# Another sharing rule for the helper operations up to tile 25, and a global transpose that is issued one place later

## The chip, the cores and the metric

The kernel runs on one core of a Trainium2 chip. A core has a matrix engine (TensorE, PE in the profile; its weight loads are the row PEld), three engines for elementwise work (VectorE or DVE, ScalarE or ACT, GpSimdE or POOL) and a queue for transfers on SyncE (SP). The metric is the device time in microseconds, the median of the runs of a kernel; lower is better.

## The reference

Two steps follow each other. First an attention over 8 batches and 8 heads with head size 64, in which each sequence has 32 global and 512 local tokens: a global query sees every key, a local query sees the 32 global keys and the local keys at most 32 positions away.

```
s_g = scale * q_g @ k_all.T            out_g = softmax(s_g) @ v_all
s_l = concat(scale * q_l @ k_g.T, where(|i-j| <= 32, scale * q_l @ k_l.T, -1e9))
out_l = softmax(s_l) @ concat(v_g, v_l)
```

Then the 8 x 544 outputs, heads side by side (512 wide), go through a dense layer with three weight matrices and a maximum, and through a second one:

```
h = max(x @ w1, x @ w2, x @ w3)        # 512 -> 768
out = h @ w_out                        # 768 -> 512
```

All data are float32.

## The kernel before

**Precision.** Outside of the first 20 tiles, a float32 operand is split in two parts: a copy rounds it to the matrix engine's fast format, and a subtraction leaves the remainder as a second operand in the same format. The matrix engine multiplies the parts (three products for the dense layers). Each split is thus one copy and one subtraction of the same width: `split_q`, `split_v`, `split_k`, `split_x`, and the same pair inside `convert` (weights, which come as 64-bit patterns of a wider type and take four VectorE instructions before the pair, lines 161 to 166), `layer1` (the hidden layer h) and `trans`/`transg`. The first 20 tiles (`NATK`, `NAT`) multiply the unsplit float32 operands, which takes no split but is slower on the matrix engine.

**Tiles.** A tile is 128 local queries of two heads of one batch; there are 128 tiles, four to a pair of heads (t = 0 to 3) and 16 to a batch. The main loop (`for i, sl in enumerate(SEQ)`) does for tile i: the transposes of the probabilities of tile i+1 (`trans`, four transposes into the only PSUM tile T, then a copy and a subtraction into the operand `pt`), some matmuls of the dense layer of the batch before (`fill(n)`: the generator in `mm[0]` issues n of them), the scores and softmax of tile i+3 (`scores`), more dense matmuls, the product with the values (`pv`), for t = 0 and 1 the scores of the global queries of the next pair (`glob`), for t = 2 their softmax (`glob_soft`), 3 dense matmuls, the transpose of the global probabilities of tile i+1 (`transg`: one transpose into a PSUM tile S, then a copy and a subtraction into columns 128 to 160 of `pt`), 7 dense matmuls, `split_v`, loads, and in the first 24 tiles a step of the weight conversion. `scores`, `glob` and `transg` share the two PSUM tiles S. A tile has 21 dense matmuls up to i = 31 and 18 after that. `pv` of a tile needs both `trans` and `transg` of that tile.

**Softmax.** `scores` reduces on VectorE (line 325), takes the exponential on ScalarE (327), adds a constant and takes the reciprocal on VectorE (330, 331), and multiplies the 128 x 192 or 128 x 224 probabilities of each of the two heads by it (`times`, lines 111 to 115). In the first 16 tiles the transposes read the result directly (tensor `early`); from tile 16 on it takes a transfer (`prob<-s`) into the operand format first.

**Who does a helper operation.** Three helpers pick their engine while the program is written: `sub` (VectorE or GpSimdE), `copy` (VectorE or ScalarE) and `times` (any of the three). `load` keeps a sum of estimated nanoseconds for each engine ("a", "d", "p"); `least` gives an operation to the engine whose sum, with the operation's cost added, is the smallest; `spend` books work with a fixed engine; `settle(4500)`, once a tile, lifts each sum to at least the largest one less 4500. GpSimdE cannot read PSUM, so operations that read PSUM are for VectorE or ScalarE. Line 97 in the profile is the instruction of `sub`, 103 and 105 are those of `copy` on VectorE and ScalarE, 111, 113 and 115 those of `times` on VectorE, ScalarE and GpSimdE. The program's order on each engine is in the main the order in which the loop issues the instructions; a list scheduler puts an instruction whose operands it expects late behind later ones that it expects ready.

Of the kernel before, what the change touches and what calls it, by code (L numbers as in the profile page):

```python
# [50 lines left out]
def f32(ap):  # L51
    return ap.bitcast(F32)


def body(ctx, tc, kin, qin, vin, min_, win, out):
# [12 lines left out]
    small = ctx.enter_context(tc.tile_pool(name="small", bufs=2))  # L68


    load = {"a": 0.0, "d": 0.0, "p": 0.0}

    def width(ap):
        n = 1
        for x in ap.shape[1:]:
            n *= x
        return n

    def spend(e, ns):
        load[e] += ns  # L80

    def least(costs):
        e = min(costs, key=lambda e: load[e] + costs[e])
        load[e] += costs[e]
        return e

    def settle(ns):
        top = max(load.values()) - ns
        for e in load:
            load[e] = max(load[e], top)  # L90

    def sub(out, a, b, psum=False):
        n = width(out)
        c = {"d": n * 1.04 + (160 if psum else 110)}
        if not psum:
            c["p"] = n * 2.32 + 130
        (dve if least(c) == "d" else pool).tensor_tensor(out=out, in0=a, in1=b, op=ALU.subtract)  # L97

    def copy(out, a, psum=False):
        n = width(out)  # L100
        c = {"d": n * (1.04 if psum else 0.52) + (160 if psum else 150), "a": n * 0.833 + (150 if psum else 190)}
        if least(c) == "d":
            dve.tensor_copy(out=out, in_=a)
        else:
            act.copy(out=out, in_=a)  # L105

    def times(out, a, col):
        n = width(out)
        e = least({"d": n * 0.52 + 125, "a": n * 0.833 + 185, "p": n * 1.27 + 150})
        if e == "d":  # L110
            dve.tensor_scalar(out=out, in0=a, scalar1=col, scalar2=None, op0=ALU.mult)
        elif e == "a":
            act.activation(out=out, in_=a, func=AF.Copy, scale=col)
        else:
            pool.tensor_scalar(out=out, in0=a, scalar1=col, scalar2=1.0, op0=ALU.mult, op1=ALU.mult)  # L115
# [13 lines left out]
    def clear():  # L129
        for t in (*probg, qgz):  # L130
            pool.memset(f32(t), 0.0)
# [3 lines left out]
    def weight(n, a):  # L135
        return wt[n][:, 512 * a:512 * a + 512]
# [17 lines left out]
    def convert(n):  # L154
        r = raw[n].bitcast(I32).rearrange("p (n t) -> p n t", t=2)
        if n < 18:
            c = spare[n // 2 % 2 if n < 15 else 1][:, n % 2]
        else:
            c = moe.tile([128, 512], I32, name="wct", tag="o", bufs=2)
        marks[n] = act.activation(out=f32(c), in_=f32(r)[:, :, 1], func=AF.Abs).ins.name  # L160
        dve.tensor_scalar(out=f32(c), in0=f32(c), scalar1=2.0 ** -15, scalar2=HIMAX, op0=ALU.max, op1=ALU.min)
        dve.tensor_scalar(out=c, in0=c, scalar1=0x07FFFFFF, scalar2=3, op0=ALU.bitwise_and, op1=ALU.logical_shift_left)
        spend("a", 520)
        yield
        dve.scalar_tensor_tensor(out=c, in0=r[:, :, 1], scalar=-0x40000000, in1=c, op0=ALU.bitwise_and, op1=ALU.bitwise_or)
        dve.scalar_tensor_tensor(out=c, in0=r[:, :, 0], scalar=29, in1=c, op0=ALU.logical_shift_right, op1=ALU.bitwise_or)
        spend("d", 1900)
        yield
        wt[n] = const.tile([128, 1024], F32R, name=f"w{n}", tag=f"w{n}")
        copy(weight(n, 0), f32(c))  # L170
        sub(weight(n, 1), f32(c), f32(weight(n, 0)))
        yield
# [20 lines left out]
    EARLY = 16  # L193
# [144 lines left out]
    def trans(sl):  # L338
        if sl >= NS:
            return  # L340
        s = sc.pop(sl)
        ps, n = turned, WIN[sl % 4][1] - 128
        pr, ident = (ps, one) if sl < EARLY else (ps.bitcast(F32R), identr)
        for j in range(2):
            pe.transpose(pr[:, 256 * j:256 * j + 128], s[:, j, 0:128], ident)  # L345
            pe.transpose(pr[0:n, 256 * j + 128:256 * j + 256], s[:, j, 128:128 + n], ident)  # L346
        src = ps.rearrange("p (x q) -> p x q", q=128)
        if sl < NAT:
            pt = pts[sl] = att.tile([128, 2, 2, 160], F32, name="pt", tag="pt")
            copy(pt.rearrange("p j c q -> p (j c) q")[:, :, 0:128], src, True)  # L350
        else:
            pt = pts[sl] = att.tile([128, 2, 2, 2, 160], F32R, name="pt", tag="pt")
            v = pt.rearrange("p j c a q -> p (j c) a q")
            copy(v[:, :, 0, 0:128], src, True)
            sub(v[:, :, 1, 0:128], src, f32(v)[:, :, 0, 0:128], True)

    def transg(sl):
        if sl >= NS:
            return
        p, t = divmod(sl, 4)  # L360
        pt = pts[sl]
        i, h, n = GCH[t]
        g = psS.tile([128, 512], F32, name="S")
        pe.transpose(g.bitcast(F32R)[:, 0:128], probg[p % 2][:, i], identr)  # L364
        src = g[:, 64 * h:64 * h + 64 * n].rearrange("p (c j g) -> p c j g", j=2, g=SG)
        if sl < NAT:
            copy(pt.rearrange("p j c q -> p c j q")[:, 0:n, :, 128:160], src, True)
            return
        v = pt.rearrange("p j c a q -> p c j a q")
        hi, lo = v[:, 0:n, :, 0, 128:160], v[:, 0:n, :, 1, 128:160]  # L370
        copy(hi, src, True)
        sub(lo, src, f32(hi), True)
# [66 lines left out]
    def layer2(hh, n, stores):  # L439
        for t in range(n // 128):  # L440
            ps = pm.tile([128, 512], F32, name="pm")
            q = 0
            for f in range(6):
                for a, w in ((0, 0), (1, 0), (0, 1)):
                    pe.matmul(ps, lhsT=hh[f][:, a, 128 * t:128 * t + 128], rhs=weight(18 + f, w), start=(q == 0), stop=(q == 17))  # L445
                    q += 1
                    if q < 18:
                        yield
            o = moe.tile([128, 512], F32, name="o", tag="o", bufs=2)
            copy(o, ps, True)  # L450
            stores(t, o)
            yield
# [3 lines left out]
    def moe_local(b):  # L456
        def st(t, o):
            r = b * TOK + SG + t * 128
            nc.sync.dma_start(out=out[r:r + 128], in_=o)
        x, hh = xs[b], []  # L460
        for c0, n in ((0, 256), (256, 256)) if b == 0 else ((0, 512),):
            yield from layer1(x, hh, c0, n)
        yield from layer2(hh, SL, st)
# [45 lines left out]
    def fill(n):  # L509
        if mm[0]:  # L510
            for _ in range(n):
                next(mm[0], None)
# [3 lines left out]
    def tile_at(i):  # L516
        return SEQ[i] if i < NS else NS
# [30 lines left out]
    for i, sl in enumerate(SEQ):  # L548
        p, t = divmod(sl, 4)
        b = p // NP  # L550
        settle(4500)
        if i % 16 == 0 and b > 1:
            fill(400)
            mm[0] = moe_local(b - 1)
        trans(tile_at(i + 1))
        first = i < 32
        fill(6 if first else 4)
        next_scores(i + 3)
        if i < 16:
            if i == 7:  # L560
                clear()
            if i in (10, 12):
                load_k((i - 2) // 2)
            if i == 14:
                split_k(5)
                load_k(6)
        elif t == 3:
            split_k(p + 2)
            load_k(p + 3)
        fill(5 if first else 4)  # L570
        pv(sl)
        if i >= 12:
            if t <= 1 or i in (12, 13):
                glob(p + 1 if i >= 16 else 4, t if i >= 16 else i - 12)
            elif t == 2 or i == 14:
                glob_soft(p + 1 if i >= 16 else 4)
        fill(3)
        if i + 1 >= EARLY:
            transg(tile_at(i + 1))
        fill(7)  # L580
        split_v(tile_at(i + 2))
        if i < 12:
            load_v(tile_at(i + 4), i + 4)
        else:
            load_v(tile_at(i + 4))
        for _ in range(WS[i] if i < len(WS) else 0):
            weight_step()
        if i < 16:
            if i % 2:
                if i < 8:  # L590
                    xs.setdefault(0, []).append(x_tile())
                split_x(xr[p][:, 2 * (i // 8):2 * (i // 8) + 2, 0:128], xs[0][p], 256 * (i // 8), 256)
            if i == 7:
                mm[0] = moe_local(0)
        elif i % 16 >= 12:
            q = b * NP + i % 16 - 12
            xs.setdefault(b, []).append(x_tile())
            split_x(xr[q][:, :, 0:128], xs[b][-1], 0, SL)
# [66 lines left out]
```

## Time and profile before

| | |
|---|---|
| median of three runs | 860.33 us (859.11 to 861.30) |
| the profiled execution, its own time | 859.92 us |
| span of its trace | 858.0 us |
| busy share of the span: PE, DVE, ACT, POOL | 95%, 74%, 59%, 61% |
| mean granted clock of the matrix engine | 0.99 |

The span is the time from the first to the last instruction of the program in the trace; the 1.92 us between it and the execution's own time lie around it. A row of a group of instructions reads: line, engine, operation, output<-inputs, shapes, xcount, then busy microseconds, the mean nanoseconds of one, and after the second bar the idle time of the engine just before these instructions and what ended it.

### The profile page before, as it was taken

How to read it: one execution, taken by the hardware profiler on the slowest of the kernel's cores; microseconds unless marked ns; L12 is line 12 of the kernel's file. 1: busy time of each engine (PE TensorE's matmuls, PEld its weight loads, DVE VectorE, ACT ScalarE, POOL GpSimd, SP SyncE). 2: the span in 40 equal slices, each digit the busy share in tenths (PEclk: the TensorE clock that was granted, in tenths of full speed). 3: DMA queues.
4: the chain of work that ended last, by engine and by line, in shares of the span. 5: the costliest groups of instructions: out<-in, count | busy, mean ns of one | idle time of the engine just before them, and what ended most of it. 6: DMA issues, size and time to landing. Idle time of an engine off the chain costs nothing.

```text
span 858.0 us, 16764 instructions
## 1 busy us (share of the span) xinstructions
PE 813.2 (95%) x4736; PEld 683.5 (80%) x4736; DVE 631.0 (74%) x2182; ACT 505.8 (59%) x1430; POOL 526.4 (61%) x695
## 2 busy tenths in 40 slices
PE   6877777999999999999999999999999999999997
PEld 5556667888888888888888888788888888777796
DVE  6999788978888887878787888787887876322111
ACT  6666566766675767676666666676667665212111
POOL 4779878766677667766776667666686656101211
PEclk9999799999999999999999999999999999999999
DMA  9843533353334333443325333433344332221000
GB/s 315 278 151 120 165 120 102 112 161 105 112 111 131 119 96 105 129 137 98 95 91 160 107 111 111 141 114 96 101 132 134 93 102 90 75 72 29 28 25 25
DMA packets 99580, 98.72 MB, mean 115 GB/s; under 512 B 21152, under 2 KB 87968, under 8 KB 99488
## 3 DMA queue, kind: packets, MB, share of 16 engines
q1 hardware_dynamic: 99344, 97.43, 36.5%
q8 instruction: 38, 0.62, 0.3%
q14 instruction: 54, 0.44, 0.2%
q10 hardware_dynamic: 144, 0.23, 0.1%
HBM read 60.39 MB, written 8.91 MB: 81 GB/s over the span
## 4 chain that ended last, share of the span: by engine, by line
PE 82%; DVE 5%; DMA 5%; POOL 4%; issue 2%; ACT 1%; SPq 0%; DVEq 0%; POOLq 0%; ACTq 0%
PE pm L424 47%; PE pm L445 16%; PE O L392 7%; PE S L322 5%; PE T L345 2%; DMA raw<-w_in 2%; PE T L346 2%; PE S L274 1%; POOL h L97 1%; DMA qn<-q_in 1%; POOL xs L97 1%; PE S L364 1%; POOL w L97 1%; POOL early L115 1%; DMA vraw<-v_in 1%
## 5 line engine op out<-in xcount | busy, mean ns | idle before, releaser
L424 PE MATMUL pm<-xs,w 128*128 128x512 f32 (+1 forms) x2160 | 501.5, 370 | 5.3 <-POOL w L97 3.8
L424 PEld LDWEIGHTS pm<-xs,w 128*128 128x128 f32 x2160 | 349.5, 191 | 56.2 <-POOL w L97 4.2
L445 PE MATMUL pm<-w,h 128*128 128x512 f32 x612 | 160.3, 399 | 1.8 <-POOL h L97 1.8
L97 POOL TENSOR_TENSOR qs<-qraw,qs 128x256 fp32r<-128x256 f32 x108 | 83.2, 770 | 75.6 <-issue 42.2
L97 POOL TENSOR_TENSOR h<-m,h 128x512 fp32r<-128x512 f32 (+1 forms) x60 | 72.3, 1205 | 87.8 <-ACT h L105 87.8
L445 PEld LDWEIGHTS pm<-w,h 128*128 128x128 f32 x612 | 107.2, 188 | 22.6 <-POOL h L97 3.7
L115 POOL TENSOR_SCALAR s<-s,z 128x224 f32<-128x224 f32 (+1 forms) x212 | 97.0, 467 | 42.8 <-ACT lox L105 18.5
L327 ACT ACTIVATE s<-s,nm 128x192 f32<-128x192 f32 (+1 forms) x224 | 103.3, 462 | 25.4 <-DVE nm L325 19.9
L433 DVE TENSOR_TENSOR m<-pm,m 128x512 f32<-128x512 f32 (+1 forms) x120 | 72.9, 607 | 49.4 <-PE pm L424 47.1
L97 DVE TENSOR_TENSOR pt<-T,pt 128x512 fp32r<-128x512 f32 x108 | 74.5, 690 | 38.8 <-ACT pt L105 36.4
L325 DVE CUSTOM_DVE_ANT_0 s<-S,mask 128x192 f32<-128x192 f32 (+1 forms) x224 | 74.6, 370 | 12.7 <-PE S L322 6.4
L97 POOL TENSOR_TENSOR vs<-vraw,vs 128x256 fp32r<-128x256 f32 x107 | 80.3, 751 | 4.9 <-ACT vs L105 4.0
L105 ACT CAST pt<-T 128x512 fp32r<-128x512 f32 x89 | 52.0, 584 | 46.9 <-PE T L346 46.8
L392 PE MATMUL O<-pt,vs 128*128 128x320 f32 (+1 forms) x432 | 77.8, 302 | 0.1
L392 PEld LDWEIGHTS O<-pt,vs 128*128 128x128 f32 x432 | 70.0, 189 | 9.3 <-DVE pt L97 0.3
L97 POOL TENSOR_TENSOR kst<-kraw,kst 64x576 fp32r<-64x576 f32 x48 | 70.6, 1471 | 5.6 <-DVE nm L325 1.5
L322 PEld LDWEIGHTS S<-kst,qs 128*128 128x128 f32 x432 | 64.4, 192 | 11.1 <-DVE nmg L278 3.2
L400 DVE TENSOR_TENSOR xr<-O,lox 64x160 f32<-64x160 f32 x216 | 67.9, 314 | 2.8
L105 ACT CAST qs<-qraw 128x256 fp32r<-128x256 f32 x90 | 36.6, 406 | 56.6 <-PE S L322 39.5
L322 PE MATMUL S<-kst,qs 128*128 128x192 f32 (+1 forms) x432 | 66.0, 275 | 1.2 <-DVE nmg L278 1.2
L398 DVE TENSOR_TENSOR lox<-O,lox 64x320 f32<-64x320 f32 x108 | 51.6, 478 | 13.4 <-ACT lox L105 7.2
L105 ACT CAST h<-m 128x512 fp32r<-128x512 f32 (+1 forms) x59 | 32.9, 558 | 40.6 <-DVE m L433 40.5
(118 smaller groups left out, 1196.4 us busy)
## 6 DMA issues: line engine op xcount, KB each, us to landing
vraw<-v_in SPq DMA_DIRECT2D x132, 128.0 KB, 2.3
qraw<-q_in SPq DMA_DIRECT2D x108, 128.0 KB, 2.2
prob<-s SPq DMA_DIRECT2D x56, 224.0 KB, 2.4
raw<-w_in SPq DMA_DIRECT2D x24, 512.0 KB, 4.8
prob<-s SPq DMA_DIRECT2D x56, 192.0 KB, 2.3
kraw<-k_in SPq DMA_DIRECT2D x27, 320.0 KB, 3.2
out_dram<-o SPq DMA_DIRECT2D x32, 256.0 KB, 2.3
qn<-q_in SPq DMA_DIRECT2D x21, 128.0 KB, 3.8
```

The costliest lines, as they stand in the source:

```text
L97: (dve if least(c) == "d" else pool).tensor_tensor(out=out, in0=a, in1=b, op=ALU.subtract)
L105: act.copy(out=out, in_=a)
L115: pool.tensor_scalar(out=out, in0=a, scalar1=col, scalar2=1.0, op0=ALU.mult, op1=ALU.mult)
L322: pe.matmul(ph[j][:, 0:n], lhsT=qs[sl][:, a, 128 * j:128 * j + 128], rhs=kst[p][:, j, c0:c0 + n], start=(a == 0), stop=(a == 1))
L325: dve.tensor_tensor_reduce(out=s[:, j, 0:n], in0=ph[j][:, 0:n], in1=mask[:, (1, 0, 1, 0)[t], 32 * (t == 0):32 * (t == 0) + n], scale=-0.12 ...
L327: act.activation(out=s[:, j, 0:n], in_=s[:, j, 0:n], func=AF.Exp, bias=nm[:, j:j + 1], scale=-1.0, accum_out=z[:, j:j + 1])
L392: pe.matmul(o[:, j, 0:320].rearrange("p (a q) -> p a q", a=2)[:, :, 0:n], lhsT=vs[sl][:, 2 * j + c].rearrange("p a d -> p (a d)"), rhs=pt[ ...
L398: dve.tensor_tensor(out=lo, in0=o[0:64, :, 160:320], in1=lo, op=ALU.add)
L400: dve.tensor_tensor(out=xr[p][64 * j:64 * j + 64, t], in0=o[0:64, j, 0:160], in1=lo[:, j], op=ALU.add)
L424: pe.matmul(ps[:, 0:n], lhsT=weight(3 * f + i, w)[:, 128 * k:128 * k + 128], rhs=xs[k][:, a, c0:c0 + n], start=(q == 0), stop=(q == 11))
L433: dve.tensor_tensor(out=m[:, 0:n], in0=ps[:, 0:n], in1=m[:, 0:n], op=ALU.max)
L445: pe.matmul(ps, lhsT=hh[f][:, a, 128 * t:128 * t + 128], rhs=weight(18 + f, w), start=(q == 0), stop=(q == 17))
```

## The change

The sums get a fourth entry "x". A cost is now booked under a string of entries: "dx" for a VectorE operation whose operands all lie in SBUF, "px" for a GpSimdE operation, "d" for a VectorE operation that reads PSUM, "a" for ScalarE. `least` takes the string for which the largest of its entries plus the cost is the smallest, and books the cost under each of them. Up to tile 25 (`shared[0]` true) this and a set of shorter costs hold; from tile 26 on only the first letter of a string counts, and the costs are those of before to within 10 ns. The second part of the weight conversion is booked under "dx". In the main loop `transg` of a tile is no longer issued between the 3 and the 7 dense matmuls of the tile before, but at the head of its own iteration, directly in front of the four transposes of the next tile.

```diff
-    load = {"a": 0.0, "d": 0.0, "p": 0.0}
+    load = {"a": 0.0, "d": 0.0, "p": 0.0, "x": 0.0}
+    shared = [True]
...
-    def spend(e, ns):
-        load[e] += ns
+    def spend(es, ns):
+        for e in es:
+            load[e] += ns
 
     def least(costs):
-        e = min(costs, key=lambda e: load[e] + costs[e])
-        load[e] += costs[e]
-        return e
+        if not shared[0]:
+            costs = {es[0]: ns for es, ns in costs.items()}
+        es = min(costs, key=lambda es: max(load[e] for e in es) + costs[es])
+        spend(es, costs[es])
+        return es[0]
...
     def sub(out, a, b, psum=False):
-        n = width(out)
-        c = {"d": n * 1.04 + (160 if psum else 110)}
+        n, k = width(out), 0 if shared[0] else 45
+        c = {"d" if psum else "dx": n * 1.04 + 75 + k + (40 if k and psum else 0)}
         if not psum:
-            c["p"] = n * 2.32 + 130
+            c["px"] = n * 2.32 + 80 + k
...
     def copy(out, a, psum=False):
-        n = width(out)
-        c = {"d": n * (1.04 if psum else 0.52) + (160 if psum else 150), "a": n * 0.833 + (150 if psum else 190)}
+        n, k = width(out), 0 if shared[0] else 75
+        c = {"a": n * 0.833 + (80 if psum else 110) + k}
+        if psum:
+            c["d"] = n * 1.04 + 80 + k
+        else:
+            c["dx"] = n * 0.52 + 75 + k
...
     def times(out, a, col):
-        n = width(out)
-        e = least({"d": n * 0.52 + 125, "a": n * 0.833 + 185, "p": n * 1.27 + 150})
+        n, k = width(out), 0 if shared[0] else 1
+        e = least({"dx": n * 0.52 + 60 + 65 * k, "a": n * 0.833 + 190, "px": n * 1.27 + 170 - 20 * k})
...
-        spend("d", 1900)
+        spend("dx", 1900)
...
         settle(4500)
+        shared[0] = i < 26
         if i % 16 == 0 and b > 1:
             fill(400)
             mm[0] = moe_local(b - 1)
+        if i >= EARLY:
+            transg(sl)
         trans(tile_at(i + 1))
...
         fill(3)
-        if i + 1 >= EARLY:
-            transg(tile_at(i + 1))
         fill(7)
```

## The prediction

> **What bounds the kernel now.** First the page, then the span cut at the tiles' borders.
>
> ```profile
> span 858.0 us, 16764 instructions
> ...
> PE 813.2 (95%) x4736; PEld 683.5 (80%) x4736; DVE 631.0 (74%) x2182; ACT 505.8 (59%) x1430; POOL 526.4 (61%) x695
> ```
>
> The table by stage has, for each stretch, its length, then the busy time and instructions of PE, PEld, DVE, ACT and POOL, the granted clock, the DMA share and rate.
>
> ```profile
> 0.00:20.00 20.00, 14.16 (x85) 11.00 (x85) 13.32 (x64) 12.18 (x36) 8.06 (x19) 1.00 0.90 310
> 20.00:80.00 60.00, 48.30 (x347) 37.73 (x346) 58.40 (x170) 39.81 (x110) 48.49 (x49) 1.00 0.60 199
> 80.00:149.00 69.00, 50.34 (x351) 46.06 (x352) 59.18 (x185) 43.28 (x124) 55.78 (x64) 0.88 0.41 126
> 149.00:170.00 21.00, 20.01 (x154) 18.60 (x153) 19.11 (x71) 16.17 (x47) 16.53 (x25) 1.00 0.39 114
> 170.00:300.00 130.00, 130.00 (x724) 109.65 (x723) 106.98 (x385) 86.45 (x250) 87.82 (x122) 1.00 0.39 122
> 300.00:728.00 428.00, 426.23 (x2369) 359.15 (x2368) 345.56 (x1238) 284.85 (x812) 290.60 (x398) 1.00 0.37 112
> ```
>
> These are two kernels. From 170 us to 728 us (tiles 30 to 127) PE idles 1.8 us of 558: only PE's own time counts there. Up to 149 us (the loop reaches tile 26) PE idles 149.0 - 112.8 = 36.2 us. VectorE is busy 130.9 us of these 149, GpSimdE 112.3, ScalarE only 95.3. Next, the normalisation in the first 80 us (minimum, median and maximum length in ns), and how long PE sat idle until it was done, ahead of the local transposes:
>
> ```profile
> L115 POOL TENSOR_SCALAR early<-early,z x30: 420/636/1109, 10.0 to 70.6; 128x224 f32<-128x224 f32 x16, 128x192 f32<-128x192 f32 x14
> ...
>   POOL early L115: 23.6, 24
> ```
>
> 23.6 of the 36.2 us are waits for the normalisation on GpSimdE. It takes 420 ns at best and 636 in the median. The same spread is in VectorE's weight conversion, four instructions for each of 24 weights (first the mean over 18 of them, then minimum, median and maximum of two of the kinds):
>
> ```profile
> L165 DVE SCALAR_TENSOR_TENSOR spare<-raw,spare 128x512 int32<-128x512 int32 x18 | 20.2, 1123 | 0.0
> L166 DVE SCALAR_TENSOR_TENSOR spare<-raw,spare 128x512 int32<-128x512 int32 x18 | 16.8, 936 | 0.0
> L162 DVE TENSOR_SCALAR spare<-spare 128x512 int32<-128x512 int32 x18 | 11.2, 628 | 0.0
> L161 DVE TENSOR_SCALAR spare<-spare 128x512 f32<-128x512 f32 x18 | 10.7, 599 | 0.2 <-ACT spare L160 0.2
> ...
> L165 DVE SCALAR_TENSOR_TENSOR spare<-raw,spare x18: 676/894/1909, 12.8 to 90.8; 128x512 int32<-128x512 int32 x18
> L161 DVE TENSOR_SCALAR spare<-spare x18: 401/578/942, 11.6 to 89.1; 128x512 f32<-128x512 f32 x18
> ```
>
> A conversion takes 1.12 + 0.94 + 0.63 + 0.60 = 3.29 us where twice 0.68 and twice 0.40 would do: 1.13 us too long, 27 us over 24 weights. The timeline shows on what:
>
> ```profile
> 43.30 1.44 POOL L97 TENSOR_TENSOR w<-spare,w 128x512 fp32r<-128x512 f32 x1 [2.53 <-ACT w L105]
> 43.79 1.49 DVE L166 SCALAR_TENSOR_TENSOR spare<-raw,spare 128x512 int32<-128x512 int32 x1
> 44.72 0.88 POOL L115 TENSOR_SCALAR early<-early,z 128x224 f32<-128x224 f32 x1
> 45.21 0.15 DVE L331 RECIPROCAL z<-z 128x1 f32<-128x1 f32 x1
> 45.65 0.14 PEld L345 LDWEIGHTS T<-one,early 128*128 128x128 f32 x1 [1.70 <-POOL early L115]
> ```
>
> L166 ends 0.54 us after the GpSimdE subtraction, which is about its own free length: one waited for the other. The normalisation stands behind the 1.44 us subtraction on GpSimdE and runs long itself, and PE waits 1.70 us for it. The Trainium skill, page "SBUF — State Buffer", section "Who interferes with whom", says that VectorE and GpSimdE share a pair of ports which one instruction holds for its whole length, while the other blocks; the trace agrees (1909 against 676 ns).
>
> **The rule, up to tile 25.** I went through the calls in program order with the costs of both rules, by arithmetic on the code alone. Up to tile 25 (the normalisations of 29 tiles among them): of 58 normalisations GpSimdE had 56 and ScalarE 1; now 13 and 42. Weight subtractions on GpSimdE go from 23 to 12, the other 11 to VectorE; so do 4 of `kst`, 5 of `xs`, 3 of `h`. The 3 global normalisations leave GpSimdE. A few copies go from VectorE to ScalarE. Prices:
>
> ```profile
> L97 POOL TENSOR_TENSOR w<-spare,w 128x512 fp32r<-128x512 f32 x18 | 25.3, 1407 | 5.5 <-ACT w L105 4.1 <-DVE w L103 1.2
> L97 POOL TENSOR_TENSOR kst<-kraw,kst 64x576 fp32r<-64x576 f32 x8 | 12.5, 1558 | 1.2 <-POOL w L97 0.6
> L97 DVE TENSOR_TENSOR w<-wct,w 128x512 fp32r<-128x512 f32 x1 | 0.7, 678 | 0.0
> L113 ACT ACTIVATE s<-s,z x11: 453/457/459, 191.5 to 677.1; 128x192 f32<-128x192 f32 x11
>   DVE z L331: 2.7, 2
>   DVE z L330: 2.4, 3
> ```
>
> GpSimdE loses 43 x 0.64 = 27.5, 11 x 1.41 = 15.5, 4 x 1.56 = 6.2, and about 10 for the eleven small ones (estimated by width from these rows): 59 of its 112 us. ScalarE gains 42 x 0.457 = 19.2, with the copies and global ones some 23: 95 + 23 = 118 us of 149. VectorE gains 11 x 0.68 = 7.5, some 7 for the other twelve subtractions and small operations by width, and gives up some 3 in copies: +12. Of its 27 us of waiting the share of GpSimdE's work that is gone (59/112 = 0.53) goes too: -14. Net -2, still about 129 us.
>
> So VectorE hardly gains, and the bounds lie apart. If VectorE must stay as idle as now (88% busy over the stage), the stage shrinks by 2/0.88, some 2 us. If it can be as full as between 20 and 80 us (58.4/60 = 0.97), the stage takes 129/0.97 = 133 us: 16 us less. PE's side says 23.6 us if each wait for GpSimdE goes, and 0.53 x 23.6 = 12.5 if they shrink as the work does. I take 10, nearer to PE's side, because PE waits for one particular operation and this is the one that moves, off the port and out of the queue of subtractions; not more, because the reciprocal still comes from VectorE (late at 45.21 above). Below nothing: the ScalarE rival. From tile 26 on the costs are nearly the old ones; the sums differ by what went before, and some copies change between ScalarE and VectorE. That costs nothing behind a PE busy 426.23 us of 428; without this cover 20 copies of about 0.6 us would be 12 us spread over two engines.
>
> **The transpose.** It issues no DMA, and is moved past seven dense matmuls, `split_v`'s copy and subtraction, the loads on SP and, on some tiles, `split_x`. What it costs on PE is read from the starts:
>
> ```profile
> 328.25 0.86 PE L424 MATMUL pm<-xs,w 128*128 128x512 f32 x3
> 328.94 0.22 PE L364 MATMUL S<-identr,probg 128*128 128x128 f32 x1
> 329.00 1.82 PE L424 MATMUL pm<-xs,w 128*128 128x512 f32 x7
> 330.66 0.22 PE L345 MATMUL T<-identr,prob 128*128 128x128 f32 x1
> ...
> 330.92 1.18 PE L424 MATMUL pm<-xs,w 128*128 128x512 f32 x4
> 331.94 0.59 PE L322 MATMUL S<-kst,qs 128*128 128x192 f32 x4
> ...
> L364 PE MATMUL S<-identr,probg x92: 220/221/223, 202.4 to 726.9; 128*128 128x128 f32 x92
> ```
>
> Three dense matmuls take 0.69 us from start to start, 0.23 each. The lone transpose takes 0.06, but the seven matmuls behind it take 1.66 instead of 1.61: 0.05 more. The four transposes take 0.26, and the four matmuls behind them 1.02 instead of 0.92. So a change from transposes back to dense matmuls costs 0.05 after one and 0.10 after four. Side by side there is one such change instead of two: at best 0.05 us a tile saved, at least nothing (if the fifth transpose adds what the lone one cost). I take 0.04, since three more transposes raised it by only 0.05: 92 x 0.04 = 3.7 us, bounds 0 and 4.6. Tiles 16 to 29 count nothing; PE has gaps there.
>
> The Trainium skill, page "TensorE: Matmul & The Clock Gate", section "Back-to-back issue gap", gives about 81 ns for each matmul of 128 columns in a stream with its weight load; the row has (0.26 + 0.10)/4 = 0.09. By the page's figure a fifth transpose would add 0.08 where the lone one costs 0.11, so 0.03 a tile and 2.8 us.
>
> What can be late is `pv`, which now follows the transpose after four dense matmuls, the scores and four more. In the trace:
>
> ```profile
> 330.83 0.29 DVE L97 TENSOR_TENSOR pt<-S,pt 128x128 fp32r<-128x128 f32 x1
> ...
> 333.31 0.74 PE L392 MATMUL O<-pt,vs 128*128 128x320 f32 x4
> ```
>
> From the transpose (328.94) to the end of its subtraction (331.12) are 2.18 us; from the transposes T (330.66) to `pv` 2.65. If the lag moves along, 0.47 us are left, so it costs nothing; behind `pv` are all dense matmuls of the tile.
>
> **Sum.** 858.0 - 10 - 3.7 = 844.3 us of span, plus 1.92 around it: 846.2. The profiled execution (859.92) lies 0.4 under the median 860.33, so 846.6 as a median; I say 846.5.
>
> **The rivals.** *Only the transpose counts*: VectorE, 97% busy from 20 to 80 us, sets the tiles' pace whoever normalises. 860.3 - 3.7 = 856.6. For it speaks the net of -2 us; against it the 23.6 us that PE waits for GpSimdE by name. *The whole wait goes*: 20 us or more early, 860.3 - 20 - 4 = 836. *ScalarE blocks (slower)*: a normalisation on ScalarE waits for the reciprocal at the head of its queue, and exponentials and PSUM copies stand behind it. In the trace twelve such instructions waited 5.1 us in five cases, 0.43 in the mean, 1.0 where they waited. With 42 waits of 1.0 us ScalarE needs 118 + 42 = 160 us for a stage of 149: 11 us longer, 860.3 + 11 - 3.7 = 867.6. It decides from (149 - 118)/42 = 0.74 us a wait. Against it: VectorE waits less for the port, so the reciprocal comes earlier, and the issue order puts other work between. *The global operand is late for `pv`*: 0.1 us over the slack costs 92 x 0.1 = 9 us, with the early gain 860.3 - 10 + 9 = 859. *The moved operations do not move what PE waits for* gives the first rival's time.
>
> **How the numbers follow.** Forecast (840 to 853) 0.56; the whole wait goes 0.12; only the transpose 0.16; ScalarE blocks 0.11; late operand 0.05. A difference under 0.3% (2.6 us, 857.7 to 862.9) is about what a measurement cannot tell from none. The first three are faster (0.84), less 0.04 for an only-transpose case with less than 2.6; ScalarE is slower 0.11, the late operand is mostly within. Faster 0.80, same 0.08, slower 0.12. The range goes from the deeper early gain (20 to 22 us and 4) at 834 past the rival at 856.6 to 860.
>
> **What would show it.** Right: up to 149 us GpSimdE busy near 53 us of it, L113 on ScalarE with about 42 more instructions, PE's wait for POOL early under 12 us, L165 and L166 nearer to 0.68, the last early tile some 10 us sooner; later the transpose next to L345 and seven matmuls taking 1.61 us. Wrong: ScalarE over 90% busy before tile 26, L345 waiting for ACT early or for z instead of POOL, or PE idle ahead of L392 waiting for pt.

## The result, and the profile after

The changed kernel takes 847.96 us (median of four runs, 845.83 to 850.40) against 860.63 us (one run more than in the table of the kernel before): a ratio of 0.9856, 95% interval 0.9826 to 0.9886, so 12.4 us less (9.8 to 15.0). The forecast was 846.5. The profiled execution took 847.44 us, with a span of 845.7.

The table by stage of the changed kernel, cut at the same times as before (length, then busy time and instructions of PE, PEld, DVE, ACT and POOL, granted clock, DMA share and rate):

```profile
0.00:20.00 20.00, 13.48 (x83) 10.26 (x84) 12.95 (x62) 11.39 (x36) 7.73 (x18) 1.00 0.90 308
20.00:80.00 60.00, 52.20 (x375) 42.61 (x373) 58.17 (x197) 52.48 (x146) 16.53 (x15) 0.94 0.70 233
80.00:149.00 69.00, 53.28 (x396) 47.26 (x396) 59.92 (x209) 53.03 (x157) 34.70 (x39) 0.95 0.38 114
...
300.00:728.00 428.00, 425.56 (x2379) 363.20 (x2378) 345.56 (x1240) 283.43 (x786) 286.25 (x396) 1.00 0.38 113
```

In the first 149 us GpSimdE is busy 59.0 us instead of 112.3, ScalarE 116.9 instead of 95.3, VectorE 131.1 instead of 130.9. PE idles 30.0 us there instead of 36.2, and does more: 852 matmuls instead of 781. From 300 to 728 us PE is as full as before. The normalisations of the first tiles by engine (minimum, median and maximum in ns, first and last start), and PE's waits for them ahead of the local transposes (us in total, times, longest), first in the changed kernel, then, in the second block, in the kernel before, for PE and for its weight loads:

```profile
L123 ACT ACTIVATE early<-early,z x20: 439/462/487, 24.7 to 68.6; 128x192 f32<-128x192 f32 x10, 128x224 f32<-128x224 f32 x10
L125 POOL TENSOR_SCALAR early<-early,z x9: 422/486/981, 10.5 to 21.5; 128x224 f32<-128x224 f32 x5, 128x192 f32<-128x192 f32 x4
...
PE T L355 <- ACT early L123: 2.7, 5, 1.5
...
PE T L355 <- POOL early L125: 0.8, 1, 0.8
```

```profile
PE T L345 <- POOL early L115: 10.1, 10, 1.6
...
PEld T L345 <- POOL early L115: 13.6, 14, 1.9
```

The prediction gave 23.6 us for the kernel before. That number is the sum of the two rows of the second block, and they show the same waits twice: in the prediction's timeline at 45.65 the weight load has waited 1.70 us, and in the same trace the matmul that it belongs to, at 45.66, 1.50. PE's own row counts once: 10.1 us before, of 36.2 idle, and now 0.8 for GpSimdE and 2.7 for ScalarE. The four conversion instructions on VectorE, of the same stretch:

```profile
L175 DVE SCALAR_TENSOR_TENSOR spare<-raw,spare 128x512 int32<-128x512 int32 x18 | 17.2, 956 | 0.0
L176 DVE SCALAR_TENSOR_TENSOR spare<-raw,spare 128x512 int32<-128x512 int32 x18 | 12.6, 701 | 0.0
...
L171 DVE TENSOR_SCALAR spare<-spare 128x512 f32<-128x512 f32 x18 | 9.5, 534 | 0.0
...
L172 DVE TENSOR_SCALAR spare<-spare 128x512 int32<-128x512 int32 x18 | 8.0, 447 | 0.0
```

Their means add up to 2.64 us instead of 3.29, where 2.15 is free of waiting (the shortest of each kind, added up). And PE's timeline in a steady tile:

```profile
309.71 0.62 PE L434 MATMUL pm<-xs,w 128*128 128x512 f32 x2
310.18 0.22 PE L374 MATMUL S<-identr,probg 128*128 128x128 f32 x1
310.24 0.23 PE L355 MATMUL T<-identr,prob 128*128 128x128 f32 x1
...
310.50 1.15 PE L434 MATMUL pm<-xs,w 128*128 128x512 f32 x4
311.48 0.60 PE L332 MATMUL S<-kst,qs 128*128 128x224 f32 x4
...
313.44 2.46 PE L434 MATMUL pm<-xs,w 128*128 128x512 f32 x10
315.74 0.22 PE L374 MATMUL S<-identr,probg 128*128 128x128 f32 x1
315.80 0.23 PE L355 MATMUL T<-identr,prob 128*128 128x128 f32 x1
...
316.09 1.16 PE L434 MATMUL pm<-xs,w 128*128 128x512 f32 x4
317.09 0.58 PE L332 MATMUL S<-kst,qs 128*128 128x192 f32 x4
```

Ten dense matmuls in a row take 2.30 us, 0.23 each with nothing over. The five transposes take 0.32 and 0.35, and the four matmuls behind them 0.06 and 0.08 too long: 0.38 and 0.43 for all, against 0.36 + 0.11 = 0.47 before.

Where the time went, by the start of the local transposes of a tile in the profiled executions:

| start of tile, us | before | changed | sooner |
|---|---|---|---|
| 26 | 148.7 | 138.5 | 10.2 |
| 32 | 180.5 | 172.3 | 8.2 |
| 112 | 643.4 | 632.0 | 11.4 |
| end of the span | 858.0 | 845.7 | 12.3 |

Eight microseconds come before tile 32, and 3.2 over tiles 32 to 112: 5.786 us a tile before, 5.746 after, 0.040 each.

The early starts are less sure than their decimals. Among the kernels of the experiments below, two pairs issue the same instructions in the same order over a long stretch: the changed one and "port counted to tile 15" up to about 90 us, where their traces start tile 16 at 76.3 and 78.9 us; "rule alone" and "transpose moved from tile 30 on" up to 164 us, where they start tile 26 at 135.0 and 137.6. So a difference of up to 2.6 us in such a start says nothing about a kernel.

### The profile page after: what moved, and what is told of

Its sections match the earlier page's. It is cut to its first block, busy times and chain, and to the rows that moved or that the text cites. A ratio compares the mean times of both kernels' runs of the same rounds, so it can differ in the third digit from the quotient of the medians.

```text
span 845.7 us, 16700 instructions
## 1 busy us (share of the span) xinstructions
PE 806.1 (95%) x4736; PEld 683.0 (81%) x4736; DVE 625.1 (74%) x2223; ACT 522.9 (62%) x1451; POOL 470.4 (56%) x633
## 4 chain that ended last, share of the span: by engine, by line
PE 77%; DVE 6%; ACT 5%; issue 4%; DMA 4%; POOL 3%; SPq 1%; POOLq 0%; DVEq 0%; ACTq 0%
PE pm L434 44%; PE pm L455 15%; PE O L402 6%; PE S L332 5%; PE T L355 2%; PE T L356 2%; POOL h L103 2%; PE S L284 1%; DMA raw<-w_in 1%; ACT s L337 1%; SPq L305 1%; DMA probg<-sg 1%; PE S L374 1%; POOL xs L103 1%; POOL w L103 1%
## 5 line engine op out<-in xcount | busy, mean ns | idle before, releaser
L434 PE MATMUL pm<-xs,w 128*128 128x512 f32 (+1 forms) x2160 | 489.4, 367 | 1.3 <-DVE m L443 0.9
L455 PE MATMUL pm<-w,h 128*128 128x512 f32 x612 | 157.4, 396 | 3.0 <-POOL h L103 2.9
L455 PEld LDWEIGHTS pm<-w,h 128*128 128x128 f32 x612 | 109.0, 188 | 23.8 <-POOL h L103 5.5
L103 POOL TENSOR_TENSOR h<-m,h 128x512 fp32r<-128x512 f32 (+1 forms) x57 | 70.3, 1234 | 102.0 <-ACT h L115 101.9
L125 POOL TENSOR_SCALAR s<-s,z 128x224 f32<-128x224 f32 (+1 forms) x197 | 86.7, 448 | 38.9 <-ACT lox L115 14.4
L115 ACT CAST pt<-T 128x512 fp32r<-128x512 f32 x108 | 63.9, 591 | 14.2 <-PE T L356 11.6
L332 PEld LDWEIGHTS S<-kst,qs 128*128 128x128 f32 x432 | 63.8, 190 | 8.5
L103 POOL TENSOR_TENSOR kst<-kraw,kst 64x576 fp32r<-64x576 f32 x45 | 65.9, 1464 | 4.5 <-DVE nm L335 1.1
L115 ACT CAST qs<-qraw 128x256 fp32r<-128x256 f32 x95 | 38.7, 407 | 41.0 <-PE S L332 28.3
```

Source lines behind the costliest of these rows:

```text
L332: pe.matmul(ph[j][:, 0:n], lhsT=qs[sl][:, a, 128 * j:128 * j + 128], rhs=kst[p][:, j, c0:c0 + n], start=(a == 0), stop=(a == 1))
L434: pe.matmul(ps[:, 0:n], lhsT=weight(3 * f + i, w)[:, 128 * k:128 * k + 128], rhs=xs[k][:, a, c0:c0 + n], start=(q == 0), stop=(q == 11))
```

## The experiments

Ratios are against the kernel before on the same chip, with 95% intervals; microseconds are that ratio of its 859.5 us.

| kernel | median us | ratio | us against before |
|---|---|---|---|
| the changed kernel | 847.96 | 0.9856 [0.9826, 0.9886] | -12.4 |
| rule alone | 851.83 | 0.9911 [0.9895, 0.9926] | -7.6 |
| transpose alone | 857.02 | 0.9973 [0.9961, 0.9985] | -2.3 |
| 58 normalisations to ScalarE, booked there | 866.86 | 1.0081 [1.0066, 1.0097] | +7.0 |
| changed, normalisations kept on GpSimdE | 862.94 | 1.0046 [1.0027, 1.0064] | +4.0 |
| two moves by hand, booked | 864.82 | 1.0061 [1.0048, 1.0074] | +5.2 |
| changed, no normalisation on GpSimdE | 851.42 | 0.9904 [0.9890, 0.9918] | -8.3 |
| changed, a dense matmul between the transposes | 850.62 | 0.9895 [0.9878, 0.9911] | -9.0 |
| changed, port counted to tile 15 | 849.00 | 0.9875 [0.9853, 0.9898] | -10.7 |
| two moves by hand, nothing else moved | 855.71 | 0.9958 [0.9946, 0.9970] | -3.6 |
| normalisations by hand, nothing else moved | 853.93 | 0.9936 [0.9923, 0.9949] | -5.5 |
| weight subtractions by hand, nothing else moved | 866.62 | 1.0080 [1.0065, 1.0094] | +6.9 |
| changed, transpose moved from tile 30 on | 849.17 | 0.9878 [0.9865, 0.9892] | -10.5 |

### Each part alone

The rule alone is the changed kernel with the transpose back in its place:

```diff
-        if i >= EARLY:
-            transg(sl)
         trans(tile_at(i + 1))
...
         fill(3)
+        if i + 1 >= EARLY:
+            transg(tile_at(i + 1))
         fill(7)
```

> The changed kernel with the global transpose back between the 3 and the 7 dense matmuls, so the sharing rule alone. If the two parts add up as the traces say (tile 32 starts 8.2 us earlier in the changed kernel, tiles 32 to 112 take 3.2 us less), this is 8 us faster than before: about 852. The rival is that the earlier transpose order is what shortened the first 30 tiles too: then less than 4 us faster, 857 or more.

The transpose alone is the kernel before with the opposite edit.

> The kernel before with the global transpose moved in front of the local ones, the old sharing rule kept. If the parts add up: 3.5 us faster, about 857, all of it after tile 30 and 30 to 40 ns a tile. If the gain per tile of the changed kernel came from the other assignment of the copies after tile 25 instead, no change: 860.5.

The rule alone gives 7.6 us, the transpose alone 2.3 (1.3 to 3.4): 9.9 together, at the lower end of what both give in the changed kernel. In the transpose's trace tile 32 starts no sooner (181.9 us) and tiles 32 to 112 take 5.747 us each, as in the changed kernel; with the rule alone they take 5.797. So the gain per tile belongs to the transpose and the early gain to the rule. The other traces agree on the first: six kernels here have the global transposes of these tiles directly in front of the local ones and take 5.733 to 5.747 us a tile, seven have them in their old place and take 5.778 to 5.806.

### Which move of the rule

First the prediction's step by itself: every local normalisation up to tile 25 to ScalarE, in the kernel before.

```diff
-        e = least({"d": n * 0.52 + 125, "a": n * 0.833 + 185, "p": n * 1.27 + 150})
+        if not late_tiles[0] and n < 544:          # late_tiles[0] = i >= 26
+            e = least({"a": n * 0.833 + 185})
+        else:
+            e = least({"d": n * 0.52 + 125, "a": n * 0.833 + 185, "p": n * 1.27 + 150})
```

> The kernel before with one thing changed: up to tile 25 every normalisation of the local probabilities is done by ScalarE (58 of them, 56 of which GpSimdE had). Theory N (PE waits for the normalisation that stands behind subtractions on GpSimdE): nearly the whole early gain, 7 to 9 us, about 852, and PE's idle time ahead of the local transposes until GpSimdE is done goes to nothing. Theory P (the port's total load sets the pace, whoever holds it): only the share of the removed GpSimdE work, 28 of 59 us, so 4 us: about 856. If ScalarE blocks: slower than 860.

And the changed kernel without it: the normalisations stay on GpSimdE, all else goes by the rule.

```diff
-        e = least({"dx": n * 0.52 + 60 + 65 * k, "a": n * 0.833 + 190, "px": n * 1.27 + 170 - 20 * k})
+        if shared[0]:
+            e = least({"px": n * 1.27 + 170})
+        else:
+            e = least({"dx": n * 0.52 + 60 + 65 * k, "a": n * 0.833 + 190, "px": n * 1.27 + 170 - 20 * k})
```

> The changed kernel with every normalisation up to tile 25 kept on GpSimdE (booked there and at the port); the rule then moves the subtractions and copies as it sees fit. Theory N: little is left of the early gain, 0 to 3 us, 854 to 857 with the transpose's share. Theory P: about half of it, 4 us, about 852.

Both are slower than the kernel before. For the first only the ScalarE rival had that, for the second no theory; and the second, which has the transpose's gain in it, is 6 us slower than the transpose alone. It is the easier to read. The rule now put most subtractions on VectorE (22 of 24 for the weights), and GpSimdE was busy 63.8 us of the first 149 instead of 112.3. A normalisation that was late only because it stands behind subtractions on GpSimdE should have become quick. Its row, PE's wait for it, and VectorE and GpSimdE around the longest one:

```profile
L128 POOL TENSOR_SCALAR early<-early,z x32: 419/732/2938, 8.8 to 75.7; 128x192 f32<-128x192 f32 x16, 128x224 f32<-128x224 f32 x16
...
PE T L358 <- POOL early L128: 10.3, 12, 2.4
...
60.28 0.68 DVE L178 SCALAR_TENSOR_TENSOR spare<-raw,spare 128x512 int32<-128x512 int32 x1
60.51 3.34 POOL L128 TENSOR_SCALAR early<-early,z 128x192 f32<-128x192 f32 x2 [4.03 <-DVE z L343]
...
60.96 0.41 DVE L174 TENSOR_SCALAR spare<-spare 128x512 f32<-128x512 f32 x1
...
61.28 0.69 DVE L179 SCALAR_TENSOR_TENSOR spare<-raw,spare 128x512 int32<-128x512 int32 x1
61.88 0.42 DVE L175 TENSOR_SCALAR spare<-spare 128x512 int32<-128x512 int32 x1
62.22 0.42 DVE L174 TENSOR_SCALAR spare<-spare 128x512 f32<-128x512 f32 x1
62.55 0.69 DVE L178 SCALAR_TENSOR_TENSOR spare<-raw,spare 128x512 int32<-128x512 int32 x1
```

It takes 732 ns in the median instead of 636, up to 2938, and PE waited for it as long as before (10.3 us against 10.1). GpSimdE had less to do and each normalisation took longer. The timeline shows on what: the longest one, the first of the two from 60.51 on, ends at 63.45, 0.21 us after the last of six conversion instructions that VectorE ran almost back to back, each at its free length of 0.4 or 0.7 us. Read with the shared port of the prediction, VectorE took it again and again, and GpSimdE waited.

The starts and ends of the traces, with each normalisation matched to its reciprocal in order, give both parts of the delay. In the kernel before, the 30 normalisations of the first tiles on GpSimdE stood 9.6 us in total behind other work of GpSimdE after their reciprocal was there, and ran 8.4 us in total beyond a free length of 0.43 us. In this experiment the first part is 0.4 us, the second 13.9.

The first kernel had a flaw of its own. The sums saw ScalarE fill up with 58 normalisations and answered by giving copies to VectorE: counted in the traces up to the start of tile 26, VectorE has 53 copies there against 22 before and 16 in the changed kernel. So the moves were made by hand, first with the booking (three of four normalisations to ScalarE, every other weight subtraction to VectorE):

```diff
+        if first26[0] and n < 544:                 # in times()
+            turn[0] += 1
+            c = {"p": c["p"]} if turn[0] % 4 == 0 else {"a": c["a"]}
...
+            if first26[0] and n == 512:            # in sub()
+                turn[1] += 1
+                del c["dp"[turn[1] % 2]]
```

> The kernel before with two moves made by hand up to tile 25, and nothing of the new sums: three of four local normalisations go to ScalarE, the fourth to GpSimdE, and the weight subtractions alternate between VectorE and GpSimdE. The transpose stays where it was. Theory T (the two moves together are the gain; each alone leaves one user of the port waiting for the other): 6 to 9 us faster than before, 851 to 853.5, as with the rule alone. Theory S (what counts is that the sums see the port, so that every small operation is placed after it): less than 3 us faster, 857 or more.

5.2 us slower than before, with 36 copies on VectorE by the same count. Then the same moves with the sums booked as before, so that every other operation stays where it was, and each of the two moves alone:

```diff
         e = least({"d": n * 0.52 + 125, "a": n * 0.833 + 185, "p": n * 1.27 + 150})
+        if first26[0] and n < 544:                 # the normalisations
+            turn[0] += 1
+            e = "p" if turn[0] % 4 == 0 else "a"
...
+        e = least(c)
+        if first26[0] and n == 512 and not psum:   # the weight subtractions
+            turn[1] += 1
+            e = "pd"[turn[1] % 2]
```

> As the kernel with the two moves by hand (three of four local normalisations to ScalarE, the weight subtractions alternating between VectorE and GpSimdE, up to tile 25), but the sums book both as before, so every other operation stays where it was; there, the sums saw ScalarE full and put 11 more copies on VectorE (31 against 20 before, 15 in the changed kernel). Theory K (the displaced copies on VectorE spoiled it; the two moves are the gain): 5 to 9 us faster than before, 851 to 855. Theory S (the moves are worth nothing unless the small subtractions and copies are placed by the port too): no faster than 858.

> Of the two moves only the normalisations (three of four to ScalarE up to tile 25), booked as before, so nothing else moves. The step of the prediction (PE waits for the normalisation on GpSimdE) gives most of the gain: 4 to 8 us faster than before, 852 to 856. If the conversion on VectorE, still waiting for the weight subtractions on GpSimdE, is what holds the tiles: less than 3 us, 857 or more.

> Of the two moves only the weight subtractions (alternating between VectorE and GpSimdE up to tile 25), booked as before. GpSimdE has 11 of them, some 15 us, less. If the normalisation is late because it stands behind subtractions on GpSimdE: 3 to 6 us faster than before, 854 to 857. If it is late because VectorE holds the port, VectorE now holding it more: no faster than before, 860 or slower.

The normalisations alone give 5.5 us (4.4 to 6.6) of the rule's 7.6, and tile 26 starts at 142.7 us, 6.0 sooner. The weight subtractions alone cost 6.9 us. Together they give 3.6. The two hand-made versions differ in little but the copies (36 on VectorE against 23), so the displaced copies cost 8.8 us (from -3.6 to +5.2), more than either part of the change gives or takes. GpSimdE's normalisations of the first tiles in the kernel before, as a group:

```profile
L115 POOL TENSOR_SCALAR early<-early,z 128x224 f32<-128x224 f32 (+1 forms) x30 | 21.0, 711 | 13.9 <-DVE identr L121 8.0 <-DVE z L330 2.5 <-PE S L318 1.9
```

The same group in the trace with the subtractions alone, and PE's wait for it:

```profile
L120 POOL TENSOR_SCALAR early<-early,z 128x224 f32<-128x224 f32 (+1 forms) x30 | 26.3, 886 | 17.0 <-DVE identr L126 8.1 <-DVE z L335 4.8 <-ACT pt L110 1.4
...
PE T L350 <- POOL early L120: 14.1, 12, 3.5
```

886 ns in the mean instead of 711, and 14.1 us of waiting on PE's row instead of 10.1, although GpSimdE has 11 subtractions of 1.4 us less. By the same sums as above, the normalisations still stand 9.1 us behind other work of GpSimdE, and run 13.7 beyond their free length. Tile 26 starts at 157.6 us, 8.9 later. Part of that loss goes with the matrix engine's clock: from 20 to 80 us it was granted 0.83 in this trace (1.00 before), and 281 matmuls kept PE busy for 47.4 us where 347 took 48.3 before. An execution of this kernel at a mean clock of 0.986 takes 864.3 us, two of the kernel before at the same clock on the same chip 859.3 and 859.5, so some 5 us remain at an equal clock. Whether the longer waits brought the lower clock, no run separates. The trace with the normalisations alone:

```profile
L119 POOL TENSOR_SCALAR early<-early,z x8: 424/452/588, 11.9 to 69.0; 128x224 f32<-128x224 f32 x4, 128x192 f32<-128x192 f32 x4
...
PE T L349 <- POOL early L119: 0.7, 1, 0.7
...
L98 POOL TENSOR_TENSOR w<-spare,w 128x512 fp32r<-128x512 f32 x18 | 27.2, 1513 | 19.8 <-ACT w L106 13.8 <-DVE w L104 4.6 <-DVE z L334 1.0
```

And the trace with both moves:

```profile
L123 POOL TENSOR_SCALAR early<-early,z x8: 428/953/2032, 11.9 to 70.7; 128x224 f32<-128x224 f32 x4, 128x192 f32<-128x192 f32 x4
...
PE T L353 <- POOL early L123: 4.2, 4, 1.7
```

With the normalisations alone, all the weight subtractions are still on GpSimdE, at 1.5 us each, and yet the eight normalisations left there take 452 ns in the median and PE waits 0.7 us for them. With half of the weight subtractions moved to VectorE as well, the same eight take 953 ns and PE waits 4.2 us. So moving subtractions to VectorE lengthens the normalisations that stay on GpSimdE, and half of the weight subtractions take next to nothing from the queue in front of them; moving the normalisation, for which PE waits, takes it out of both.

That leaves 2.1 us between the normalisations alone and the whole rule, of which the intervals (4.4 to 6.6 and 6.4 to 9.0) say little. In the rule the subtractions of `kst`, `xs` and `h` move too and VectorE gives up copies (16 against 22); which of these makes up for the weight subtractions was not tried.

### How far to go

No normalisation at all on GpSimdE, in the changed kernel:

```diff
+        if shared[0]:
+            del c["px"]                            # in times()
```

> The changed kernel, but up to tile 25 the local and global normalisations may not go to GpSimdE (13 local ones did): the rule places them on ScalarE or VectorE. If a normalisation on GpSimdE is slow because VectorE holds the port (864 ns in the mean where GpSimdE had little else to do), PE's remaining waits for it go and this is 1 to 3 us faster than the changed kernel, 845 to 847. If ScalarE is full by then: 1 to 5 us slower, 849 to 853.

3.5 us slower than the changed kernel, and the intervals just do not overlap (0.9890 and 0.9886). ScalarE is no fuller by it: ScalarE and VectorE are busy 115.0 and 129.4 us of the first 149 against 116.9 and 131.1. Tile 16 starts at 81.5 us instead of 76.3, of which up to 2.6 can be the difference between two executions. The granted clock of the first 149 us is 0.91 in this trace and 0.95 in the changed kernel's, and the execution at a mean clock of 0.990 takes 849.3 us, the changed kernel's at 0.988 and 0.991 take 850.4 and 847.4. So the size of this loss is unsure, and its cause is not shown.

The port counted to tile 15 only (`shared[0] = i < 16`):

> The changed kernel with the port counted only up to tile 15. In the changed kernel tile 16 starts 4.2 us earlier than before and tile 26 10.2 us earlier, so by then the port matters as much in tiles 16 to 25 (weight conversion goes on to tile 25): about 4 us slower than the changed kernel, 852. If the direct read of the normalised probabilities by the transposes (only up to tile 15) is what makes it matter: no more than 1 us slower, 849.

849.0 us, a ratio of 0.9875 where the changed kernel has 0.9856: no difference that can be told, and the intervals are wide enough to hold most of the 4 us of the other expectation. In its trace, of the longest of its five executions, tile 16 starts 1.6 us sooner than before, tile 26 4.6 and tile 30 4.8. Whether the rule does anything in tiles 16 to 25 stays open.

### The transpose

One dense matmul between the global transpose and the local ones:

```diff
         if i >= EARLY:
             transg(sl)
+            fill(1)
         trans(tile_at(i + 1))
         first = i < 32
-        fill(6 if first else 4)
+        fill((6 if first else 4) - (i >= EARLY))
```

> The changed kernel with one dense matmul between the global transpose and the four local ones (taken from the four that follow). If the saving after tile 30 is the second change back from transposes to dense matmuls, the lone transpose costs 0.11 us again and this is 2.5 to 4 us slower than the changed kernel, 850.5 to 852. If the saving comes from the later place of the copies on ScalarE and VectorE: no difference, 848.

```profile
311.43 0.22 PE L374 MATMUL S<-identr,probg 128*128 128x128 f32 x1
311.49 0.44 PE L434 MATMUL pm<-xs,w 128*128 128x512 f32 x1
311.77 0.22 PE L355 MATMUL T<-identr,prob 128*128 128x128 f32 x1
...
312.02 0.93 PE L434 MATMUL pm<-xs,w 128*128 128x512 f32 x3
312.78 0.60 PE L332 MATMUL S<-kst,qs 128*128 128x224 f32 x4
```

The matmul between takes 0.28 instead of 0.23: the 0.05 of the lone transpose is back. Tiles 32 to 112 take 5.769 us each, 0.023 more than in the changed kernel and 0.017 less than before. The median is 2.7 us above the changed kernel's, as expected of the second change back, but the intervals overlap a little (0.9878 and 0.9886), so the timeline carries this more than the times.

The transpose moved only from tile 30 on, since the rule alone had reached tile 26 at 135.0 us:

> The changed kernel with the global transpose moved only from tile 30 on. With the rule alone tile 26 starts 3.5 us earlier than in the changed kernel (135.0 against 138.5 us), but tile 30 at the same time. If that lead can be kept: 1 to 3 us faster than the changed kernel, 845 to 847. If the matrix engine's own work sets tile 30 by then: no difference, 848.

849.17 us, no difference that can be told from the changed kernel. Tile 26 starts at 137.6 us and tile 32 at 174.8. Up to there the instructions are those of the rule alone, so the lead of 3.5 us that the expectation starts from was in the main the difference between two executions. No version tried here beats the changed kernel.

## Why the prediction was right, point by point

**Two kernels in one.** Right: what the rule gives lies before tile 32, and what the transpose gives after it.

**The counts.** GpSimdE's early work went to 59.0 us (53 worked out), ScalarE's to 116.9 (118), VectorE's stayed at 131.1 (129). Of the 58 local normalisations ScalarE has 42 instead of 1, as worked out. A conversion waits 0.49 us instead of 1.13: 15.6 us less over 24, where 14 were put down.

**The early gain, 10 us.** The wait that the prediction named is the one that went, but its size was misread, and the 10 us came near by luck. The row of 23.6 us adds PE's waits and those of its weight loads, which are the same waits; PE's own row has 10.1. Put right, PE's side would have said 10.1 us if each wait goes and 0.53 x 10.1 = 5.4 if they shrink as the work does. The 10, taken somewhat below the 12.5 of the misread row, was thus nearly the whole wait. The rule alone measures 7.6 us (6.4 to 9.0), and PE's wait went from 10.1 to 0.8 for GpSimdE and 2.7 for ScalarE, 6.6 less. Tile 26 starts 10.2 us sooner and tile 32 8.2, each uncertain by 2 to 3 us. Two signs that the prediction had named for being wrong came up too, both small: the 2.7 us for ScalarE, and waits of PE ahead of `pv` for the subtraction into `pt` that VectorE makes, 4.4 us where the kernel before has no such wait, 2.7 us with the rule alone and 0.8 with the transpose alone. The latter is the largest wait left after the first load. The rows of PE's waits in the first 149 us:

```profile
PE S L328 <- DMA qn<-q_in: 4.7, 1, 4.7
PE O L402 <- DVE pt L103: 4.4, 5, 2.2
PE T L355 <- DMA prob<-s: 3.6, 4, 1.7
PE T L355 <- ACT early L123: 2.7, 5, 1.5
```

**Why the normalisation was late.** This step gave two reasons, that it moves "off the port and out of the queue of subtractions". Both hold in the kernel before, 8.4 us in total for the port (time beyond the free length) and 9.6 us for the queue. What does not hold is that removed subtractions are a gain by themselves. The prediction counted them on both sides, for the queue on GpSimdE and for VectorE's waits; on VectorE they hold the port against GpSimdE in turn. The 11 weight subtractions alone made the kernel 6.9 us longer and the normalisation 886 ns instead of 711; with all of them left, and most normalisations gone, the time fell by 5.5. In the Trainium skill, page "SBUF — State Buffer", section "Who interferes with whom", it is the order of issue that decides which of the two blocks. The runs show that either can be the one that waits (VectorE's conversions of 3.29 us before, normalisations of 886 ns after the move); the order of issue itself was not varied.

**VectorE stays full.** Its early busy time did not shrink (130.9 to 131.1 us), and PE gained nevertheless. The rival drawn from that, that only the transpose counts (856.6), is refuted by the rule alone at 851.83.

**ScalarE blocks.** It did not in the changed kernel: its normalisations take 462 ns in the median of the first tiles, and one later form waited 1.2 us for the reciprocal over 11 instructions, 0.11 each where 0.74 was the point from which it decides (1.7 us over all 44 on ScalarE in the first 149 us, two global ones among them). The rival's price of up to 11 us was near what the two booked versions lost (5.2 and 7.0 us), but by another road: copies displaced to VectorE (shown for the first of them alone).

```profile
L123 ACT ACTIVATE s<-s,z 128x224 f32<-128x224 f32 x11 | 5.0, 477 | 1.2 <-DVE z L340 0.7 <-DVE z L341 0.5
```

**The transpose, 3.7 us at 0.04 a tile.** The tiles show 0.040 (5.786 to 5.746 us); the runs of the transpose alone 2.3 us (1.3 to 3.4), which is less than 92 x 0.040 = 3.7; in its trace tile 32 starts 1.4 us later than before. The global operand was not late for `pv` in the steady tiles, where PE's busy time stayed at 425.6 of 428 us. The Trainium skill, page "TensorE: Matmul & The Clock Gate", section "Back-to-back issue gap", gives about 81 ns for a matmul of 128 columns in a stream; the two tiles quoted above have 0.38/5 and 0.43/5 = 0.08. The saving of 2.8 us that the prediction worked out from this figure lies within the interval of the runs, the 3.7 that went into the sum just above it.

**The sum.** Both parts were put too high, 10 for 7.6 and 3.7 for 2.3. The changed kernel gains 12.4 us (9.8 to 15.0) where its parts alone give 9.9, so the forecast came nearer as a whole than in its terms.

## What to carry to other kernels

When two engines take turns at one resource, ask first which of their operations is awaited by the engine that sets the end, and take that one off the resource: it gave 5.5 of 7.6 us here, while moving other work from one of the two to the other cost 6.9. Before a wait is priced, see which rows its total adds up: an engine's instructions and its weight loads can wait for the same thing at the same time (10.1 us here, not 23.6). An automatic sharing rule that is told of one more burden will answer somewhere else (8.8 us here), so an experiment on one move has to hold the rest still. Short matmuls cost less side by side than strewn among long ones; what a stray one costs is read from the start times of the long ones behind it.

## What was not expected of the hardware

A GpSimdE instruction with a free length of 420 ns took up to 2938 ns while VectorE worked on SBUF operands, and its mean rose (711 to 886 ns) as GpSimdE's own load fell (112.3 to 97.2 us of the first 149). A lone transpose between dense matmuls costs PE 0.06 us itself and 0.05 more in the matmul behind it; after five in a row that surcharge is 0.06 to 0.08, hardly more than after one (0.10 after four in the tile that the prediction shows).
